# A decode step of attention and an FFN: the first keys on ScalarE's DMA queue, and round 0's product in two pieces

## The chip, the cores and the metric

The kernel runs on one core of a Trainium2 chip. The metric is the device time of one execution in microseconds. The kernel before has a median of 677.2 us over three runs (676.89 to 677.97). All data are float32 and lie in the device's memory (HBM) before the run starts.

## The reference

One decode step for a batch of two. `x` is 2x1x448. The result mixes an attention over a cache of keys and values with a two-layer FFN, by a gate that is computed from `x`:

```
q      = (x @ wq) as 16 heads of 256
scores = q . k_cache / sqrt(256)        # k_cache: 2 x 16 x 4096 x 256
p      = softmax(scores)
a      = (p . v_cache) @ wo             # v_cache: 2 x 16 x 4096 x 256
h      = relu(x @ w1 + b1) ** 2         # 448 -> 1792
b      = h @ w2 + b2                    # 1792 -> 448
g      = sigmoid(sum(x * gate_w))
out    = g * a + (1 - g) * b
```

Keys and values are 134.2 MB each; `wq` and `wo` are 7.3 MB each, `w1` and `w2` together 6.4 MB.

## The kernel before, in words

The work is cut into 16 rounds. A round is a pair of heads of one batch entry: 8.39 MB of keys, laid as 128 partitions of 64 keys x 256 numbers (a row of 64 KB in each partition), and as much of values. In a round VectorE multiplies the keys by the query (in place, line 213), sums over the 256 numbers (line 222) and finds the maxima (223, 224); ScalarE takes the exponentials (240); TensorE multiplies the values by them (`values`, into `po`), sums them (`sums`) and turns the result for the last product with `wo` (`turn`).

Three large buffers in SBUF hold everything that is loaded: `keys[0]`, `keys[1]` and `vals`, 64 KB in each partition. At the start they serve other ends:

- `keys[1]` first receives `wq` with a small pack behind it (`x` transposed, the gate's weights, `b1`). TensorE computes all queries from it (banks `pq`, the semaphore value `TE_Q1` marks that `wq` is read), and only then may the keys of round 1 (k1) be loaded there.
- `keys[0]` receives the keys of round 0 (k0).
- `vals` first receives `wf`, which is `w1` and `w2`. TensorE computes the FFN's first layer from `w1` (into `fin`, then turned into `sm`), VectorE adds the bias, applies the squared relu and multiplies by 1 - g (lines 215 to 218, giving `hT`), and TensorE multiplies `hT` by `w2` into `acc`. The value `TE_ADD` marks that `wf` is read, and only then may the values of round 0 (v0) be loaded into `vals`.

The order of the work is written out by hand, one instruction stream for each engine; semaphores couple them. All big transfers are issued by SyncE (SP), through its one DMA queue, in this order: `wq`, k0, `wf`, k1 (waits for `TE_Q1`), v0 (waits for `TE_ADD`), k2 (waits for round 0's sum on VectorE, since `keys[0]` is then free), v1 (waits for round 0's values on TensorE), and so on in pairs. ScalarE issues one small transfer at the start, the bias `b2` (1.8 KB, line 171). Each round's keys count up the semaphore of their buffer, `KL[0]` or `KL[1]`.

After `wq` has landed, SP has nothing to do with the queries: DVE copies the pack (174), forms the gate's sum, TensorE makes 32 matmuls into the two banks `pq`, ScalarE copies them (182), TensorE spreads them over the partitions and ScalarE copies the eight query tiles `qb` (184). Round 0 of VectorE waits for the first tile.

Of the kernel before, what the change touches and what calls it, by code (L numbers as in the profile page):

```python
# [7 lines left out]
ALU = mybir.AluOpType  # L8
AX = mybir.AxisListType

P = 128
# [23 lines left out]
def gated_mix_kernel(nc, b2, wq, wf, wo, k_cache, v_cache, out):  # L35
    B, H, S, DH = k_cache.shape
# [5 lines left out]
    KEYS = 2 * S // P  # L42
# [11 lines left out]
    pe, dve, act, pool, sp = nc.tensor, nc.vector, nc.scalar, nc.gpsimd, nc.sync  # L54
# [3 lines left out]
    def sb(name, *free):  # L58
        return nc.alloc_sbuf_tensor(name, [P, *free], F32)[:]
# [4 lines left out]
    keys = [sb("k0", PLACE), sb("k1", PLACE)]  # L64
# [29 lines left out]
    DV, AC, TE, GP = (Count(nc, n) for n in ("dve", "act", "pe", "pool"))  # L94
    KL = [Count(nc, "k0_landed"), Count(nc, "k1_landed")]
# [14 lines left out]
    def kv(cache, r):  # L110
        t, b = rounds[r]
        return cache[b, 2 * t:2 * t + 2].rearrange("h (p j) d -> (h p) (j d)", j=KEYS)

    def load(dst, src, sem, after=None):
        ins = sp.dma_start(dst, src)  # L115
        if after:
            after[0].on(ins, after[1])
        return sem.up(ins, 16)
# [10 lines left out]
    def te_mt(r):  # L129
        return TE_MT0 if r == 0 else TE_SUM0 + 4 * (r - 1) + 3  # L130
# [4 lines left out]
    def te_val(r):  # L135
        return TE_SUM0 + 4 * r + 1
# [29 lines left out]


    load(keys[1][:, :3 * N + N // 2 + PK], wq[:, :3 * N + N // 2 + PK], QL)
    load(keys[0], kv(k_cache, 0), KL[0])
    load(vals[:, :spare], wf, FL)  # L170
    BL.up(act.dma_start(b2r, b2), 16)


# [17 lines left out]
    def turned(r):  # L191
        t, b = rounds[r]
        OC.up(TE.on(act.activation(o, po, AF.Copy), te_val(r)))  # L193
        AC_OT[r] = AC.up(TE.on(act.activation(oT[:, t, :, b, :], ot[:, :NJ * 2].rearrange("p (j h) -> p j h", h=2), AF.Copy), te_ot(r)))  # L194

    def normed(r):
        b = rounds[r][1]
        n = DV.up(TE.on(dve.reciprocal(rc, sm[:, :2]), te_sum(r)))
        RL.up(DV.on(dve.scalar_tensor_tensor(rl, rc.unsqueeze(1).to_broadcast([P, 2, 2]), gP[:, 0, b:b + 1],
                                             sel.rearrange("p (s h) -> p s h", s=2), op0=ALU.mult, op1=ALU.mult), n))  # L200

    def k_view(r):
        return keys[r % 2].rearrange("p (j d) -> p j d", d=DH)

    load(keys[1], kv(k_cache, 1), KL[1], (TE, TE_Q1))
    for r, (t, b) in enumerate(rounds):
        kt = k_view(r)
        q = qb[:, (t // 2) * B + b, (t % 2) * DH:(t % 2 + 1) * DH]
        if r < 4:
            dve.wait_ge(AC.h, AC_QB[(t // 2) * B + b])  # L210
        elif r == 4:
            dve.wait_ge(AC.h, AC_QB[-1])
        n = DV.up(KL[r % 2].on(dve.tensor_tensor(kt, kt, q.unsqueeze(1).to_broadcast([P, KEYS, DH]), op=ALU.mult), 16 * (r // 2 + 1)))  # L213
        if r == 0:
            DV_H = DV.up(TE.on(dve.tensor_tensor(hb, sm[:, :FC * B].rearrange("p (c b) -> p c b", b=B), b1T.unsqueeze(2).to_broadcast([P, FC, B]), op=ALU.add), TE_PT))
            DV_H = DV.up(DV.on(dve.tensor_scalar(hb, hb, 0.0, None, op0=ALU.max), DV_H))
            DV_H = DV.up(DV.on(dve.tensor_mul(hT, hb, hb), DV_H))
            DV_H = DV.up(DV.on(dve.tensor_tensor(hT, hT, gP[:, 1, :].unsqueeze(1).to_broadcast([P, FC, B]), op=ALU.mult), DV_H))
            load(vals, kv(v_cache, 0), VL, (TE, TE_ADD))
        else:  # L220
            normed(r - 1)
        DV_S = DV.up(DV.on(dve.tensor_reduce(s, kt, axis=AX.X, op=ALU.add), n))  # L222
        MX.up(DV.on(dve.tensor_reduce(m, s, axis=AX.X, op=ALU.max), DV_S))
        DV_NB = DV.up(TE.on(dve.tensor_reduce(nb, mt[:, :64], axis=AX.X, op=ALU.max, negate=True), te_mt(r)))  # L224
        if r > 0:
            turned(r - 1)
            if r < R - 1:
                load(vals, kv(v_cache, r), VL, (TE, te_val(r - 1)))
            else:
                for i, (lo, hi) in enumerate(zip(WO_CUTS, WO_CUTS[1:])):  # L230
                    load(vals[:, lo * D:hi * D], wo[:, lo * D:hi * D], WL[i], (TE, te_val(r - 1)) if i == 0 else None)
        if r + 2 < R:
            load(keys[r % 2], kv(k_cache, r + 2), KL[r % 2], (DV, DV_S))
        elif r + 2 == R:
            at = V_CUT * DH
            load(keys[r % 2][:, :at], kv(v_cache, R - 1)[:, :at], VT[0], (DV, DV_S))
            load(keys[r % 2][:, at:], kv(v_cache, R - 1)[:, at:], VT[1])
        for hh in range(2):
            z = slice(64 * hh, 64 * hh + 64)
            e = act.activation(p8[z, :, hh:hh + 3:2], s[z].rearrange("p (m s) -> p m s", s=2), AF.Exp,  # L240
                               bias=nb[z], accum_out=rsm[z, hh:hh + 1])
            if hh == 0:
                DV.on(e, DV_NB)
            else:
                EX.up(e)
# [71 lines left out]
    def add(lt, rhs):  # L317
        n = added[0]
        g = 32 * (n % 4)
        added[0] += 1  # L320
        return mm(acc[g:g + B, :D], lt, rhs, n < 4, n >= n_acc - 4)
# [47 lines left out]
    pe.wait_ge(BL.h, 16)  # L369
    pe.wait_ge(DV.h, DV_H)  # L370
    add(gP[0:1, 1, :], b2r)
# [21 lines left out]
    for i, (t, k) in enumerate(blocks):  # L393
# [9 lines left out]
        n = i - early  # L403
# [72 lines left out]
```

## Time and profile before

| | |
|---|---|
| median of three runs | 677.2 us |
| the profiled execution | 676.97 us |
| its span, first to last instruction | 675.6 us |
| bytes read from HBM | 289.55 MB |
| busy: VectorE, TensorE, ScalarE | 566.4 us (84%), 215.6 us (32%), 36.2 us (5%) |
| the data queue's packets | 5772 with 289.56 MB, 99.2% of 16 DMA engines' span |
| mean granted TensorE clock | 0.653 |

The page shows one profiled execution. "Span" is the time from its first to its last instruction, and the profiled execution's own time has 1.4 us around it. The share of the DMA queue is the time that its packets took on the core's 16 DMA engines, as a share of the span. A row of the timeline gives the start in us, the duration, the engine (SPq and ACTq are the engines' own sequencers, here issuing DMAs), the line, the operation with its tile and the number of instructions merged into it, and in brackets the idle time before it with what ended it. In the names, `k` stands for either keys buffer, `v` for `vals`.

### The profile page before, as it was taken

To read this page: it belongs to the slowest core of one execution; us is meant where nothing else is said; L and a number is where in the kernel's file an instruction comes from. 1 tells how busy PE (TensorE), PEld (TensorE's weight loads), DVE (VectorE), ACT (ScalarE), POOL (GpSimd) and SP (SyncE) were. 2 spreads that over 40 slices of the span, in tenths; PEclk is the share of its full clock that TensorE was granted. 3 is DMA by queue.
4 is the path that set the end of the run, shared out by engine and by line. 5 is a ranking of instruction groups with operands and counts; after the bars stand their busy time and mean duration, and the time that the engine had idled before them with its cause. 6 is when DMAs were issued, how large, how long until landed. Compare 5 with 4: busy or idle time off the path is not lost. (4 is left out here: it accounts for less than half of the span.)

```text
span 675.6 us, 3473 instructions
## 1 busy us (share of the span) xinstructions
PE 215.6 (32%) x1522; PEld 67.6 (10%) x1522; DVE 566.4 (84%) x120; ACT 36.2 (5%) x111; POOL 2.1 (0%) x15
## 2 busy tenths in 40 slices
PE   0726141150605124060503305050421405051357
PEld 0201000010101101010100101010010101011012
DVE  1066999999989797998979798997979799797960
ACT  0121000000000000000000000000000000000000
POOL 1000000000000000000000000000000000000000
PEclk9976666575756657585755658575565858565579
DMA  9999999999999999999999999999999999999997
GB/s 381 431 453 421 435 435 436 435 431 435 435 435 435 435 431 435 435 435 435 435 435 435 435 435 435 431 435 435 435 431 435 435 435 435 435 435 435 423 418 293
DMA packets 5779, 289.63 MB, mean 429 GB/s; under 512 B 653, under 2 KB 782, under 8 KB 1038
## 3 DMA queue, kind: packets, MB, share of 16 engines
q1 hardware_dynamic: 5772, 289.56, 99.2%
q8 instruction: 3, 0.05, 0.0%
q14 instruction: 2, 0.02, 0.0%
q10 hardware_dynamic: 2, 0.00, 0.0%
HBM read 289.55 MB, written 0.00 MB: 429 GB/s over the span
## 5 line engine op out<-in xcount | busy, mean ns | idle before, releaser
L213 DVE TENSOR_TENSOR k<-k,q 128x16384 f32<-128x16384 f32 x16 | 275.6, 17223 | 51.7 <-DMA k<-in_k_cache_dram 51.7
L222 DVE TENSOR_REDUCE s<-k 128x64 f32<-128x16384 f32 x16 | 275.4, 17212 | 0.0
L274 PE MATMUL po<-v,p 128*4 128x512 f32 x960 | 137.4, 737 | 291.4 <-PEq L278 291.4
L274 PEld LDWEIGHTS po<-v,p 128*4 128x4 f32 x960 | 26.6, 99 | 389.5 <-issue 389.5
L274 PE MATMUL mt<-ident,m 128*64 128x64 f32 x64 | 7.7, 334 | 88.8 <-PEq L278 88.8
L193 ACT ACTIVATE o<-po 128x512 f32<-128x512 f32 x16 | 9.6, 597 | 449.8 <-PE po L274 449.8
L274 PE MATMUL ot<-rl,o 128*128 128x2 f32 x128 | 16.4, 250 | 15.6 <-PEq L278 15.6
L274 PEld LDWEIGHTS ot<-rl,o 128*128 128x128 f32 x128 | 15.5, 191 | 30.0 <-issue 30.0
L240 ACT ACTIVATE p<-s,nb 64x64 f32<-64x64 f32 x32 | 11.2, 350 | 104.8 <-DVE nb L224 104.6
L274 PE MATMUL sm<-rsm,ones 128*128 128x2 f32 x32 | 8.9, 348 | 21.2 <-PEq L278 21.2
L274 PEld LDWEIGHTS mt<-ident,m 128*64 128x64 f32 x64 | 5.2, 205 | 90.4 <-issue 90.4
L174 DVE COPY pk<-k 128x28 f32<-128x28 f32 x1 | 0.2, 179 | 16.5 <-DMA k<-in_wq_dram 16.5
L224 DVE TENSOR_REDUCE nb<-mt 128x1 f32<-128x64 f32 x16 | 3.6, 224 | 10.6 <-PE mt L274 10.6
L274 PE MATMUL fin<-v,pk 128*2 128x448 f32 x32 | 6.0, 933 | 16.6 <-DMA v<-in_wf_dram 16.6
L274 PEld LDWEIGHTS sm<-rsm,ones 128*128 128x128 f32 x32 | 8.0, 310 | 23.8 <-issue 23.8
L258 DVE COPY wide<-oT 128x2 f32<-128x2 f32 x8 | 0.7, 162 | 10.4 <-ACT oT L194 10.4
L274 PE MATMUL pq<-k,pk 128*2 128x512 f32 x64 | 9.3, 747 | 0.0
L274 PE MATMUL po<-k,p 128*4 128x512 f32 x64 | 8.7, 702 | 0.0
L274 PE MATMUL sm<-ys,ones 128*128 128x2 f32 x2 | 0.6, 350 | 21.0 <-DVE ys L177 21.0
L261 DVE COPY y<-fin 128x112 f32<-128x112 f32 x1 | 0.3, 275 | 7.7 <-PE fin L274 7.7
L240 ACT ACTIVATION_READ_ACCUMULATOR p<-s,nb 64x1 f32 x32 | 5.9, 184 | 0.0
L274 PE MATMUL acc<-v,oT 128*2 128x448 f32 x48 | 4.9, 538 | 0.4 <-ACT oT L194 0.3
(59 smaller groups left out, 58.2 us busy)
## 6 DMA issues: line engine op xcount, KB each, us to landing
k<-in_wq_dram SPq DMA_DIRECT2D x1, 7182.0 KB, 19.6
v<-in_wf_dram SPq DMA_DIRECT2D x1, 6272.0 KB, 52.8
k<-in_v_cache_dram SPq DMA_DIRECT2D x1, 6144.0 KB, 37.8
v<-in_wo_dram SPq DMA_DIRECT2D x1, 3584.0 KB, 18.6
k<-in_v_cache_dram SPq DMA_DIRECT2D x1, 2048.0 KB, 42.4
v<-in_wo_dram SPq DMA_DIRECT2D x1, 1792.0 KB, 22.6
v<-in_wo_dram SPq DMA_DIRECT2D x1, 896.0 KB, 24.3
v<-in_wo_dram SPq DMA_DIRECT2D x1, 672.0 KB, 25.4
```

The lines of the kernel that those rows point to most:

```text
L174: DV_PK = DV.up(QL.on(dve.tensor_copy(pk, keys[1][:, 3 * N + N // 2:3 * N + N // 2 + PK]), 16))
L193: OC.up(TE.on(act.activation(o, po, AF.Copy), te_val(r)))
L213: n = DV.up(KL[r % 2].on(dve.tensor_tensor(kt, kt, q.unsqueeze(1).to_broadcast([P, KEYS, DH]), op=ALU.mult), 16 * (r // 2 + 1)))
L222: DV_S = DV.up(DV.on(dve.tensor_reduce(s, kt, axis=AX.X, op=ALU.add), n))
L224: DV_NB = DV.up(TE.on(dve.tensor_reduce(nb, mt[:, :64], axis=AX.X, op=ALU.max, negate=True), te_mt(r)))
L240: e = act.activation(p8[z, :, hh:hh + 3:2], s[z].rearrange("p (m s) -> p m s", s=2), AF.Exp, bias=nb[z], accum_out=rsm[z, hh:hh + 1])
L258: DV_W = dve.tensor_copy(wide[:, n, 0:W:16], o_block(t, k))
L261: DV_Y4 = DV.up(TE.on(dve.tensor_copy(y4, fin[:, :DQ]), TE_FIN))
L274: return pe.matmul(dst, lt, rhs, start=start, stop=stop)
```

## The change

Two edits. The first takes k0's load from SP's queue and has ScalarE issue it, ahead of the transfer of `b2`; SP issues `wq` and behind it at once `wf`. The second cuts round 0's product (the multiplication of the keys by the query) in two: 48 of the 64 keys of each partition, then the four steps of the FFN's first layer, then the other 16 keys. Rounds 1 to 15 keep their product in one piece. Semaphores and what they count stay as they were.

```
-    load(keys[0], kv(k_cache, 0), KL[0])
     load(vals[:, :spare], wf, FL)
+    KL[0].up(act.dma_start(keys[0], kv(k_cache, 0)), 16)
     BL.up(act.dma_start(b2r, b2), 16)
...
-        n = DV.up(KL[r % 2].on(dve.tensor_tensor(kt, kt, q.unsqueeze(1).to_broadcast([P, KEYS, DH]), op=ALU.mult), 16 * (r // 2 + 1)))
+        cut = 48 if r == 0 else KEYS
+
+        def times_q(lo, hi):
+            return DV.up(KL[r % 2].on(dve.tensor_tensor(kt[:, lo:hi], kt[:, lo:hi], q.unsqueeze(1).to_broadcast([P, hi - lo, DH]), op=ALU.mult), 16 * (r // 2 + 1)))
+
+        n = times_q(0, cut)
         if r == 0:
             DV_H = DV.up(TE.on(dve.tensor_tensor(hb, sm[:, :FC * B].rearrange("p (c b) -> p c b", b=B), b1T.unsqueeze(2).to_broadcast([P, FC, B]), op=ALU.add), TE_PT))
             DV_H = DV.up(DV.on(dve.tensor_scalar(hb, hb, 0.0, None, op0=ALU.max), DV_H))
             DV_H = DV.up(DV.on(dve.tensor_mul(hT, hb, hb), DV_H))
             DV_H = DV.up(DV.on(dve.tensor_tensor(hT, hT, gP[:, 1, :].unsqueeze(1).to_broadcast([P, FC, B]), op=ALU.mult), DV_H))
+            n = times_q(cut, KEYS)
             load(vals, kv(v_cache, 0), VL, (TE, TE_ADD))
```

Two places in the order of instructions change. The first is the start of SP's stream, which is the order of its DMA queue (`in_wq`, `in_wf` and the caches are the sources; `pe` and `dve` are the engines whose semaphores a row waits for). Before, and then with the change:

```order
L115 DMA k<-in_wq_dram 128x14364 [waits barrier_Pool_Activation_PE_DVE_SP_release]
L115 DMA k<-in_k_cache_dram 128x16384
L115 DMA v<-in_wf_dram 128x12544
L115 DMA k<-in_k_cache_dram 128x16384 [waits pe]
L115 DMA v<-in_v_cache_dram 128x16384 [waits pe]
```

```order
L115 DMA k<-in_wq_dram 128x14364 [waits barrier_Pool_Activation_PE_DVE_SP_release]
L115 DMA v<-in_wf_dram 128x12544
L115 DMA k<-in_k_cache_dram 128x16384 [waits pe]
L115 DMA v<-in_v_cache_dram 128x16384 [waits pe]
L115 DMA k<-in_k_cache_dram 128x16384 [waits dve]
```

The second row of before, k0, is gone from SP's stream. It now stands at the head of ScalarE's, where `b2` was first, ahead of the load of the activation table. The other place is round 0 on VectorE (`k` is the keys buffer, `hb` and `hT` the FFN's hidden layer, `s` the scores). Before, and then with the change:

```order
L213 TENSOR_TENSOR k<-k,q 128x16384 [waits act,k0_landed]
L215 TENSOR_TENSOR hb<-sm,pk 128x28 [waits pe]
L216 TENSOR_SCALAR hb<-hb 128x28 [waits dve]
L217 TENSOR_TENSOR hT<-hb 128x28 [waits dve]
L218 TENSOR_TENSOR hT<-hT,gP 128x28 [waits dve]
L222 TENSOR_REDUCE s<-k 128x64 [waits dve]
```

```order
L216 TENSOR_TENSOR k<-k,q 128x12288 [waits act,k0_landed]
L220 TENSOR_TENSOR hb<-sm,pk 128x28 [waits pe]
L221 TENSOR_SCALAR hb<-hb 128x28 [waits dve]
L222 TENSOR_TENSOR hT<-hb 128x28 [waits dve]
L223 TENSOR_TENSOR hT<-hT,gP 128x28 [waits dve]
L216 TENSOR_TENSOR k<-k,q 128x4096 [waits k0_landed]
L228 TENSOR_REDUCE s<-k 128x64 [waits dve]
```

A quarter of the product now stands behind the four steps of the FFN and ahead of the sum.

## Prediction

> **What bounds the kernel now.** I read the page's DMA rows first, then the chain that ended last, then the rounds in the timeline, then the first 95 us.
>
> ```profile
> q1 hardware_dynamic: 5772, 289.56, 99.2%
> q8 instruction: 3, 0.05, 0.0%
> q14 instruction: 2, 0.02, 0.0%
> ...
> DMA 4%; PE 2%; SPq 0%; DVE 0%; issue 0%
> ```
>
> One queue carries all the data, and its packets fill 99.2% of the sixteen DMA engines' span. The chain that ended last is short and names a transfer as its longest part. VectorE's 84% looks like a bound, so the rounds must decide. Two of them late in the run:
>
> ```profile
> 558.99 8.54 PE L274 MATMUL po<-v,p 128*4 128x512 f32 x64 [20.70 <-PEq L278]
> ...
> 578.23 17.23 DVE L213 TENSOR_TENSOR k<-k,q 128x16384 f32<-128x16384 f32 x1 [2.86 <-DMA k<-in_k_cache_dram]
> ...
> 597.68 9.67 PE L274 MATMUL po<-v,p 128*4 128x512 f32 x64 [20.69 <-PEq L278]
> ...
> 616.93 17.22 DVE L213 TENSOR_TENSOR k<-k,q 128x16384 f32<-128x16384 f32 x1 [2.87 <-DMA k<-in_k_cache_dram]
> ```
>
> A round takes 616.93 - 578.23 = 38.70 us. Keys and values of a round are 16.78 MB, so 433 GB/s. VectorE idles 2.87 us in each, for the keys to land; it could do a round in 35.8. So the end is set by bytes in the queue. The change moves no byte more or less: it can only alter the time by making the queue start earlier, run at another rate, or run empty.
>
> The first 95 us hold everything that moves:
>
> ```profile
> 0.73 0.51 ACTq L171 DMA_DIRECT2D b2r<-in_b_dram  x1
> ...
> 0.74 0.39 SPq L115 DMA_DIRECT2D k<-in_wq_dram  x1
> ...
> 1.19 0.41 SPq L115 DMA_DIRECT2D k<-in_k_cache_dram  x1
> ...
> 1.64 0.43 SPq L115 DMA_DIRECT2D v<-in_wf_dram  x1
> ...
> 20.31 0.18 DVE L174 COPY pk<-k 128x28 f32<-128x28 f32 x1 [16.48 <-DMA k<-in_wq_dram]
> ...
> 30.92 0.33 SPq L115 DMA_DIRECT2D k<-in_k_cache_dram  x1
> ...
> 31.94 0.60 ACT L184 ACTIVATE q<-ot 128x512 f32<-128x512 f32 x1 [0.42 <-PE ot L274]
> ...
> 36.03 1.88 PE L274 MATMUL pq<-v 128*128 128x512 f32 x4
> ...
> 39.63 17.23 DVE L213 TENSOR_TENSOR k<-k,q 128x16384 f32<-128x16384 f32 x1 [17.63 <-DMA k<-in_k_cache_dram]
> ...
> 54.48 6.05 PE L274 MATMUL fin<-v,pk 128*2 128x448 f32 x32 [16.56 <-DMA v<-in_wf_dram]
> ...
> 62.30 0.19 DVE L215 TENSOR_TENSOR hb<-sm,pk 128x28 f32<-128x28 f32 x1 [5.44 <-PE sm L274]
> ...
> 62.95 0.19 DVE L218 TENSOR_TENSOR hT<-hT,gP 128x28 f32<-128x28 f32 x1
> 63.06 17.21 DVE L222 TENSOR_REDUCE s<-k 128x64 f32<-128x16384 f32 x1
> ...
> 68.99 0.33 SPq L115 DMA_DIRECT2D v<-in_v_cache_dram  x1
> 80.30 0.33 SPq L115 DMA_DIRECT2D k<-in_k_cache_dram  x1
> ...
> 81.33 17.21 DVE L213 TENSOR_TENSOR k<-k,q 128x16384 f32<-128x16384 f32 x1
> ...
> 94.32 8.77 PE L274 MATMUL po<-v,p 128*4 128x512 f32 x64 [11.29 <-PEq L278]
> ...
> 117.07 17.21 DVE L213 TENSOR_TENSOR k<-k,q 128x16384 f32<-128x16384 f32 x1
> ```
>
> The landings stand one behind the other: wq 20.3, k0 39.6, wf 54.5, v0 94.3. Each later issue is ahead of need: k1 leaves at 30.92, v0 at 68.99, k2 at 80.30. When a new transfer's packets begin, the fine windows of the same trace show (the last column is GB/s; sixteen packets begin together, so a burst marks the begin of a row on most engines):
>
> ```profile
> 1.00:1.60 0.60, 0.00 (x0) 0.00 (x0) 0.54 (x2) 0.32 (x1) 0.50 (x2) 1.00 0.00 0
> 1.60:2.60 1.00, 0.00 (x0) 0.00 (x0) 0.89 (x3) 0.96 (x1) 1.00 (x8) 1.00 2.70 921
> ...
> 53.20:54.20 1.00, 0.00 (x0) 0.00 (x0) 1.00 (x1) 0.00 (x0) 0.00 (x0) 0.50 2.43 1049
> 54.40:58.00 3.60, 3.52 (x20) 0.69 (x24) 2.46 (x1) 0.00 (x0) 0.00 (x0) 0.50 0.67 291
> ...
> 70.20:70.80 0.60, 0.00 (x0) 0.00 (x0) 0.60 (x1) 0.00 (x0) 0.00 (x0) 1.00 3.53 1529
> 72.60:73.20 0.60, 0.00 (x0) 0.00 (x0) 0.60 (x1) 0.00 (x0) 0.00 (x0) 1.00 3.54 1529
> 75.00:75.60 0.60, 0.00 (x0) 0.00 (x0) 0.60 (x1) 0.00 (x0) 0.00 (x0) 0.50 3.27 1420
> ```
>
> The first data flow 0.9 to 1.9 us after the issue at 0.74: that is the lead a transfer needs. A row of keys (64 KB) takes 2.4 us on an engine, 70.2 to 72.6 to 75.0. Eight rows make a transfer (128 partitions on 16 engines), so k1's rows begin at 53.2 to 54.2 and v0's at 72.6 to 73.2, both without a gap.
>
> **The change part by part.**
>
> *k0 on ScalarE's queue.* Now wq and k0 are in flight together. No row shows two data queues at once, so I bound the time W at which wq lands. From below it is 20.3, if k0 takes nothing from it; from above 39.6, when before both had landed. A fair share puts wq near the upper end, so I work with 39.6, the dearest: 19.3 us later than before. Everything that hangs on wq moves by 19.3.
>
> k1's issue: 30.92 + 19.3 = 50.2, data 51.1 to 52.1. Its place begins at 53.2. Cost 0, with 1.1 us to spare; wf's bytes, which SP has queued behind wq, are the cover. Without wf, the queue would lie empty from 39.6 to about 51.6, 12 us.
>
> [...]
>
> *The product in two pieces.* The first query tile is ready at 31.94 + 0.60 + 19.3 = 51.8. By then k0 is there. 48 of 64 keys take 17.23 x 48/64 = 12.9 us, to 64.8. TensorE ends its query work at 36.03 + 1.88 + 19.3 = 57.2; wf has landed by 54.5; `fin` takes 6.05, then 62.30 - 60.53 = 1.8 us to the bias: 65.0. So both arrive together, 65.0, where before it was 62.3. The four steps take 62.95 + 0.19 - 62.30 = 0.84, to 65.9. From there to v0's issue before: 68.99 - 63.14 = 5.85, now 71.7. Data flow from 72.6 to 73.6, where they were needed at 72.6 to 73.2: cost 0 to 1.0 us. I take 0, since W = 39.6 was the dearest case. Here the cut is the cover: in one piece the product would end at 69.0, v0 be issued at 75.7 and the engines stand idle for 3.4 to 5 us.
>
> *TensorE's clock.* The first layer ran at a granted clock of 0.50 (54.40 to 58.00 in the windows), 17 us after the query work. [...]
>
> *The second piece and what is late next.* 4.3 us behind the steps: 70.2, sum to 87.4, so k2 leaves at 87.4 instead of 80.30. Its data follow v0's eight rows, 72.6 + 8 x 2.41 = 91.9 at the earliest, and need up to 1.9 us of lead: 2.6 us to spare. The exponentials of round 0 are 7.1 us later too, at 88.5, while v0 lands at 94.3. VectorE needs 117.07 - 81.33 = 35.74 for a round where the queue needs 38.70, so the 7.1 us are gone after three rounds. Splitting adds one instruction, off the path.
>
> *ScalarE's order.* One issue more ahead of `b2` and the table load, some 0.4 to 0.5 us at 0.7, where ScalarE then waits for wq; b2, now behind k0, is wanted at 65.9. Both 0.
>
> *The rate.* While both queues run, from 2 to 38 us, the rate may differ. Above: wq's 7.35 MB landed at 20.3, and at the 433 GB/s of the rounds they take 17.0; of the 3.3 us at the start, 0.74 precede the issue and 0.9 the first data, so at most 1.6 can be won by a second queue that fills gaps. Below, the slowest stretch of these is that of k0, 420 GB/s:
>
> ```profile
> 20.20:39.60 19.40, 16.88 (x82) 5.16 (x82) 0.68 (x4) 6.15 (x11) 0.00 (x0) 1.00 0.97 420
> ...
> 54.40:94.20 39.80, 13.80 (x78) 3.69 (x78) 33.56 (x9) 2.70 (x6) 0.00 (x0) 0.63 0.98 422
> 94.20:132.90 38.70, 10.83 (x78) 3.52 (x78) 37.97 (x7) 1.65 (x6) 0.00 (x0) 0.63 1.00 434
> ```
>
> 420 for 434 over 36 us is 1.2 us. (The 39.80 us for k1 and v0, 1.1 more than a round, are no price of the short lead: the bursts at 70.2, 72.6 and 75.0 are unbroken. I put them down to the few packets of the instruction queues in the first rows.) Nearest is the row of k0 alone: 0.
>
> Sum: 676.97 + 0 + 0 + 0 = 677.0 for the profiled execution, bounds -1.6 and +1.0 + 1.2. The profiled execution lies 0.2 under the median, so I say 677.1.
>
> **The rivals.**
>
> *The start is filled better.* For it: 3.3 us pass before the rate is full, and one late engine costs 1.1 behind wf. Against it: the same sixteen engines work, and neither issue is earlier than 0.73. All of the 1.6 gives 675.6; with the 1.1 gone too, 674.5.
>
> *The query chain comes too late.* The mechanism: sharing costs rate, so wq lands after 39.6, and SP, which issues in order, holds k1 and behind it v0. k1's place is at 53.2 and the chain from W to its data 10.6 + 1.9 us, so it decides from W = 40.7. With the 1.2 us of rate, which put W at 40.8, and the 1.0 of v0 that is 679.3; each further us of W adds one.
>
> *The transfers do not mix.* One queue may be served first. If wq, the start is as before but for k2 at 62.95 + 0.19 + 4.3 + 17.2 = 84.7, still ahead of 91.9; if k0, W is 39.6 and the sum above holds. Either way 677.1.
>
> **How the numbers follow.** A measurement of this kernel tells 0.2%, 1.4 us, from no change. No effect by the full queue: 0.60; the transfers do not mix: 0.06; better start: 0.15, of which I count all as faster; query chain too late: 0.19, slower. Faster 0.15, same 0.66, slower 0.19. The range, 675.4 to 679.3, reaches the full gain of the start and the price of the late chain.
>
> **What would show it.** Right: wq's copy (line 174) begins at 37 to 40, k1 leaves at 48 to 50.5, v0 before 72, and bursts at 2.4 us steps run through 53 and 73; the values of round 0 still begin at about 94.3, and the rounds stay at 38.70. Wrong: a stretch without packets near 52 or 73, values of round 0 later than 95.5, or a landing of wf well off 54.5. A change of the rounds' 38.70 would break the argument as a whole.

## The result, and the profile after

The change makes the kernel slower: 678.6 us median over 22 runs (677.33 to 679.94) against 677.14 us for the kernel before, run beside it as often (676.76 to 678.24). The ratio is 1.0019, with a 95% interval of 1.0013 to 1.0025, so 1.3 us, 0.9 to 1.7 (it goes by all the runs; the two medians lie 1.46 us apart). The forecast was no change.

From the page of the changed kernel, the second DMA queue and the chain that ended last:

```profile
q10 hardware_dynamic: 146, 8.39, 2.9%
...
DMA v<-in_wo_dram 4%; PE po L280 1%; PE fin L280 0%; SPq L115 0%; DVE y L267 0%
```

The second queue carries k0's 8.39 MB and the end is still a chain behind a transfer. The bound has not moved, so I looked for a time in which the queue moved nothing. The start of its timeline:

```profile
39.60 0.18 DVE L174 COPY pk<-k 128x28 f32<-128x28 f32 x1 [35.78 <-DMA k<-in_wq_dram]
...
50.15 0.33 SPq L115 DMA_DIRECT2D k<-in_k_cache_dram  x1
...
51.87 12.96 DVE L216 TENSOR_TENSOR k<-k,q 128x12288 f32<-128x12288 f32 x1 [10.58 <-ACT q L184]
...
57.08 3.19 PE L280 MATMUL fin<-v,pk 128*2 128x448 f32 x32
...
60.93 1.05 PE L280 MATMUL sm<-ident,o 128*128 128x8 f32 x10 [0.66 <-ACT o L186]
64.75 0.18 DVE L220 TENSOR_TENSOR hb<-sm,pk 128x28 f32<-128x28 f32 x1
...
65.40 0.19 DVE L223 TENSOR_TENSOR hT<-hT,gP 128x28 f32<-128x28 f32 x1
...
65.73 1.65 PE L280 MATMUL acc<-b2r,gP 1*2 1x448 f32 x2 [3.76 <-DVE hT L223]
...
67.31 5.80 PE L280 MATMUL acc<-v,hT 128*2 128x448 f32 x28
...
73.16 0.33 SPq L115 DMA_DIRECT2D v<-in_v_cache_dram  x1
...
94.99 9.49 PE L280 MATMUL po<-v,p 128*4 128x512 f32 x64 [5.04 <-PEq L284]
```

wq lands at 39.6, k1 leaves at 50.15, round 0's product starts at 51.87: all as forecast. The view of the DMA issues gives the time from issue to landing (last column):

```profile
k<-in_wq_dram SPq DMA_DIRECT2D x1, 7182.0 KB, 38.8
k<-in_k_cache_dram ACTq DMA_DIRECT2D x1, 39.1
```

wq and k0 were issued together and landed 0.3 us apart, so the two shared the engines and neither was served first. v0 leaves at 73.16 and not at 71.7. Fine windows of the same trace show what that does (the third column from the right is the granted TensorE clock, the last GB/s):

```profile
53.20:54.20 1.00, 1.00 (x4) 0.49 (x3) 1.00 (x1) 0.74 (x2) 0.00 (x0) 1.00 2.43 1049
55.60:56.60 1.00, 1.00 (x4) 0.38 (x2) 1.00 (x1) 0.74 (x2) 0.00 (x0) 1.00 2.42 1049
71.80:72.60 0.80, 0.80 (x8) 0.08 (x2) 0.80 (x1) 0.00 (x0) 0.00 (x0) 0.50 0.20 82
72.60:73.40 0.80, 0.51 (x4) 0.00 (x0) 0.80 (x1) 0.00 (x0) 0.00 (x0) 0.97 0.01 0
...
74.00:74.80 0.80, 0.00 (x0) 0.00 (x0) 0.80 (x1) 0.00 (x0) 0.00 (x0) 1.00 3.78 1311
76.80:77.60 0.80, 0.00 (x0) 0.00 (x0) 0.80 (x1) 0.00 (x0) 0.00 (x0) 0.50 3.02 1311
62.00:65.60 3.60, 0.00 (x0) 0.00 (x0) 3.50 (x6) 0.17 (x1) 0.00 (x0) 0.56 0.92 400
62.40:62.60 0.20, 0.00 (x0) 0.00 (x0) 0.20 (x1) 0.00 (x0) 0.00 (x0) 0.51 0.00 0
65.60:73.20 7.60, 7.38 (x30) 1.08 (x30) 7.57 (x2) 0.00 (x0) 0.00 (x0) 0.54 0.86 371
```

k1's rows begin at 53.2 and again 2.4 us later: no gap there. But v0's rows, which began at 72.6 to 73.2 before, begin at 74.0 to 74.8, with no row in the window from 72.6 to 73.4. That is a hole of 1.4 us, and the next row follows after 2.8 us instead of 2.4, so the refill costs some 0.4 more. The last three rows show why v0 was late. TensorE had nothing to do from 62.0 to 65.7, its granted clock fell to 0.50 at 62.4 (0.56 on the mean of that time), and it computed the FFN's second layer at 0.54 on the mean, in 7.4 us; the clock was back only at 72.6, when the layer was all but done.

The hole stays to the end. The values of round 1 and of round 14, in the kernel before and then in the changed one:

```profile
133.27 9.77 PE L274 MATMUL po<-v,p 128*4 128x512 f32 x64 [14.49 <-PEq L278]
...
636.41 9.09 PE L274 MATMUL po<-v,p 128*4 128x512 f32 x64 [20.72 <-PEq L278]
```

```profile
134.91 8.30 PE L280 MATMUL po<-v,p 128*4 128x512 f32 x64 [9.22 <-PEq L284]
...
638.04 9.32 PE L280 MATMUL po<-v,p 128*4 128x512 f32 x64 [20.70 <-PEq L284]
```

1.64 us later in round 1, 1.63 in round 14: no round gives any of it back or adds to it. The profiled execution took 678.82 us, 1.85 more than that of before.

### The profile page after: what moved, and what is told of

The parts are those of the page before. It is cut to its first block, busy times and chain, and to the rows that moved or that the text cites. A ratio compares the mean times of both kernels' runs of the same rounds, so it can differ in the third digit from the quotient of the medians.

```text
span 677.5 us, 3474 instructions
## 1 busy us (share of the span) xinstructions
PE 216.7 (32%) x1522; PEld 67.7 (10%) x1522; DVE 566.4 (84%) x121; ACT 36.1 (5%) x111; POOL 2.1 (0%) x15
## 3 DMA queue, kind: packets, MB, share of 16 engines
q10 hardware_dynamic: 146, 8.39, 2.9%
## 5 line engine op out<-in xcount | busy, mean ns | idle before, releaser
L216 DVE TENSOR_TENSOR k<-k,q 128x16384 f32<-128x16384 f32 (+2 forms) x17 | 275.7, 16219 | 39.5 <-DMA k<-in_k_cache_dram 28.9
L280 PE MATMUL po<-v,p 128*4 128x512 f32 x960 | 139.6, 746 | 266.8 <-PEq L284 266.8
L280 PE MATMUL acc<-v,hT 128*2 128x448 f32 x28 | 5.8, 923 | 0.0
## 6 DMA issues: line engine op xcount, KB each, us to landing
v<-in_wf_dram SPq DMA_DIRECT2D x1, 6272.0 KB, 53.2
```

Of the source, the lines that this page charges most:

```text
L216: return DV.up(KL[r % 2].on(dve.tensor_tensor(kt[:, lo:hi], kt[:, lo:hi], q.unsqueeze(1).to_broadcast([P, hi - lo, DH]), op=ALU.mult), 16 ...
L280: return pe.matmul(dst, lt, rhs, start=start, stop=stop)
```

## The experiments

The theory after reading the trace: v0 is issued after the queue has run empty, since the FFN's steps wait for 48 keys of product that start 12 us later, and since TensorE's clock falls meanwhile. Rivals: two queues cost by themselves; the cut costs by itself; the second layer is slow because of what runs beside it. All times are in us; each ratio is to the kernel before run in the same session, with its 95% interval. e1 has five runs, e5 four, the others eleven. Those runs of the kernel before had a median of 677.12 in the first session, 677.59 in the second and 678.02 in the third.

| run | median (range) | ratio to before |
|---|---|---|
| e1, queue only | 682.1 (681.46 to 683.61) | 1.0072 (1.0058 to 1.0086) |
| e2, cut only | 676.96 (676.78 to 678.02) | 0.9993 (0.9984 to 1.0002) |
| e3, cut at 32 | 677.68 (676.83 to 678.51) | 1.0004 (0.9995 to 1.0013) |
| e4, TensorE kept busy | 677.71 (676.78 to 678.94) | 1.0008 (0.9999 to 1.0017) |
| e5, cut at 56 | 680.26 (679.97 to 680.81) | 1.0044 (1.0029 to 1.0060) |
| e6, before, end kept busy | 677.1 (676.88 to 677.43) | 0.9996 (0.9987 to 1.0005) |
| e7, e4 with e6's edit | 677.29 (676.83 to 678.18) | 0.9996 (0.9987 to 1.0005) |
| e8, the change with e6's edit | 678.71 (677.04 to 679.22) | 1.0014 (1.0005 to 1.0023) |
| e9, e7 with k1 later | 678.94 (678.37 to 679.98) | 1.0015 (1.0006 to 1.0025) |
| e10, e7 with early matmuls | 677.68 (677.10 to 677.99) | 1.0000 (0.9991 to 1.0009) |

### e1: the queue alone

```
-        cut = 48 if r == 0 else KEYS
+        cut = KEYS
...
-            n = times_q(cut, KEYS)
```

> The first edit alone: k0 on ScalarE's queue, round 0's product in one piece. Theory (v0 is issued too late and the DMA queue runs empty): the product runs from 51.9 to 69.1, the FFN's steps to 70.0, its second layer at half clock 7.6 us, v0's issue at 77.5, first data at 78.4 instead of 72.7: a hole of 5.7 us and 0.6 for the refill, so 677.1 + 6 = about 683 us. Rival (sharing the DMA engines between two queues costs by itself, the product's cut does nothing): 678.6.

```profile
69.52 1.65 PE L279 MATMUL acc<-b2r,gP 1*2 1x448 f32 x2 [8.02 <-DVE hT L223]
...
76.25 0.33 SPq L115 DMA_DIRECT2D v<-in_v_cache_dram  x1
```

682.1, where the theory had 683 and the rival 678.6. In the timeline TensorE waits 8.02 us for the FFN's steps, v0 leaves at 76.25. Without the cut the first edit costs 5 us; the cut buys most of it back.

### e2: the cut alone

```
     load(keys[1][:, :3 * N + N // 2 + PK], wq[:, :3 * N + N // 2 + PK], QL)
+    load(keys[0], kv(k_cache, 0), KL[0])
     load(vals[:, :spare], wf, FL)
-    KL[0].up(act.dma_start(keys[0], kv(k_cache, 0)), 16)
```

> The second edit alone: k0 back on SP's queue between wq and wf, the product cut at 48. Theory: v0's issue stays at 69.0, since the FFN's first layer waits for wf and not for the product; k2 leaves at 84.7, still ahead of its place at 92: 677.1, no change. Rival (the cut costs by itself, or the later k2 does): about 678.6.

```profile
69.34 0.33 SPq L115 DMA_DIRECT2D v<-in_v_cache_dram  x1
83.72 0.33 SPq L115 DMA_DIRECT2D k<-in_k_cache_dram  x1
...
94.25 9.49 PE L280 MATMUL po<-v,p 128*4 128x512 f32 x64 [7.79 <-PEq L284]
```

No change, as the theory said. The later k2 (83.72 for 80.30) costs nothing, and v0's values begin at 94.25 (94.32 before).

### e3: the cut after 32 keys

```
-        cut = 48 if r == 0 else KEYS
+        cut = 32 if r == 0 else KEYS
```

> The changed kernel with the cut after 32 keys instead of 48. Theory: the first piece ends at 51.9 + 8.7 = 60.6, before the first layer is done at 62.0, so the FFN's steps run from 62.0 to 62.9; TensorE has idled about 1 us and keeps its clock, the second layer takes 3.5 to 4.2 us, v0's issue at 66.4 to 67.1, no hole at 73: 677.1. Rival (two queues cost by themselves): 678.6.

```profile
62.19 0.91 PE L280 MATMUL acc<-b2r,gP 1*2 1x448 f32 x2 [1.04 <-DVE hT L223]
...
63.02 4.87 PE L280 MATMUL acc<-v,hT 128*2 128x448 f32 x28
...
67.94 0.33 SPq L115 DMA_DIRECT2D v<-in_v_cache_dram  x1
```

The first piece is done at 59.7, VectorE waits for the first layer and not the other way round, TensorE idles 1.04 us ahead of the second, v0 leaves at 67.94 and the loss is gone, to within the measurement. k0 is still on ScalarE's queue. The second layer took 5.8 us, more than my 3.5 to 4.2: a pause of 1.04 us did not keep the clock, which stood at 0.71 on the mean from 62.2 to 68.0.

### e4: the cut at 48, TensorE kept busy

```
     done(ins, TE_PT)
+    for n in range(16):
+        g = 32 * (n % 4)
+        mm(pq[0][g:g + B, :D], xT[:, 0, :], vals[:, (n % 4) * D:(n % 4 + 1) * D])
     pe.wait_ge(BL.h, 16)
```

> The changed kernel, cut at 48, with sixteen extra matmuls behind the first layer, whose results go unused, so that TensorE does not idle from 62.0 to 65.7. Theory (the half clock after that idle time is what made v0 late): the second layer takes 3.5 to 4.2 us instead of 7.5, v0's issue at 69.1 to 69.8 instead of 73.2, no hole: 677.1. Rival (the second layer is slow because it runs beside VectorE's multiplication and the loads): it stays at 7.5 us, v0's issue at 73.2, 678.6.

```profile
60.93 3.19 PE L280 MATMUL pq<-v,pk 128*2 128x448 f32 x32
...
64.75 0.91 PE L280 MATMUL acc<-b2r,gP 1*2 1x448 f32 x2 [0.64 <-DVE hT L223]
...
65.59 3.17 PE L280 MATMUL acc<-v,hT 128*2 128x448 f32 x28
...
68.81 0.33 SPq L115 DMA_DIRECT2D v<-in_v_cache_dram  x1
```

```profile
64.60:68.80 4.20, 4.01 (x30) 0.82 (x30) 4.20 (x2) 0.00 (x0) 0.00 (x0) 1.00 1.15 499
72.60:73.40 0.80, 0.00 (x0) 0.00 (x0) 0.80 (x1) 0.00 (x0) 0.00 (x0) 1.00 2.84 1229
```

This run decides between the causes of the slow second layer. VectorE multiplies beside it as in the changed kernel, and the loads run; only TensorE's idle time is filled. The clock stays at 1.00, the layer takes 4.0 us instead of 7.4, and v0's rows begin at 72.6 as before. From the end of the FFN's steps to v0's issue it is 4.2 us here and in the profiles of e7, e9 and e10, which have the same sixteen matmuls. The time returns to 677.71, level with before as far as the interval tells.

### e5: a larger dose

```
-        cut = 48 if r == 0 else KEYS
+        cut = 56 if r == 0 else KEYS
```

> The changed kernel with the cut after 56 keys instead of 48: a dose. Theory (v0's lateness is paid one for one once the queue is empty): the first piece ends 2.15 us later, the second layer is at half clock again, v0's issue at about 75.3 in place of 73.2, and the time 2.1 us above the changed kernel's 678.6: 680.7. Rival (the cost is one of sharing, or of the second queue): 678.6.

```profile
74.49 0.33 SPq L115 DMA_DIRECT2D v<-in_v_cache_dram  x1
```

Between the profiled executions of the change, e5 and e1, v0 leaves at 73.16, 74.49 and 76.25, and they took 678.82, 680.18 and 681.80: steps of 1.33 and 1.76 in the issue, 1.36 and 1.62 in the time. Once the queue was empty, lateness was paid about one for one. v0 left 0.8 us before the 75.3 that I expected, since the layer did not run as long at half clock (its groups of weight loads are 0.75 us apart up to 72.56 and 0.38 from 73.15 on): 6.45 us from its first matmul to v0's issue, for 7.43 in the changed kernel.

### e6, e7, e8: the end kept busy

The profiled execution of e2 took 677.56 although its rounds ran level with before. Its end and that of the kernel before:

```profile
666.00:668.00 2.00, 2.00 (x12) 0.30 (x9) 0.54 (x8) 0.00 (x0) 0.00 (x0) 0.50 0.96 401
```

```profile
666.00:668.00 2.00, 2.00 (x28) 0.52 (x20) 0.00 (x0) 0.00 (x0) 0.00 (x0) 1.00 0.93 387
```

In e2 TensorE fell to 0.50 just ahead of the products with `wo`, after a pause of 0.97 us and small matmuls, and they took 6.32 us:

```profile
665.90 6.32 PE L280 MATMUL acc<-v,oT 128*2 128x448 f32 x48 [0.26 <-ACT oT L194]
```

The 22 runs of the kernel before lie in two groups, twelve at 676.76 to 677.20 and ten at 677.59 to 678.24. To see whether that is this clock, e6 fills the pause in the kernel before, e8 in the changed kernel and e7 in e4:

```
+    for n in range(4):
+        mm(pq[0][32 * n:32 * n + B, :], xT[:, 0, :], keys[R % 2][:, n * QB:(n + 1) * QB])
     done(turn(), te_ot(R - 1))
```

> The kernel before with four extra matmuls, whose results go unused, between the last values and the last turn, where TensorE idles about 1 us. Theory (the runs of before lie in two groups, near 676.8 and near 677.9, because TensorE sometimes drops to half clock between 664 and 670 us, as in the profile of the cut alone): the upper group vanishes, all runs at 676.7 to 677.0. Rival (the groups come from the transfers): two groups as before, median 677.1.

> The changed kernel with TensorE kept busy in both places: sixteen extra matmuls behind the first layer and four ahead of the last turn. If two queues cost nothing by themselves and the end's clock is the only noise left: 676.8, level with the kernel before that has the four. If sharing has a price of its own, some tenths more: 677.1 to 677.4.

> The changed kernel with the four extra matmuls ahead of the last turn only. Theory (two causes: v0's late issue at the start, the clock at the end): the start's cost stays, 1.0 to 1.7 us above the kernel before that has the four, so 677.8 to 678.5, and the runs spread less than the changed kernel's 677.3 to 679.9. Rival (the changed kernel's cost sits at the end): 676.8.

```profile
663.48 1.03 PE L274 MATMUL pq<-k,pk 128*2 128x512 f32 x8
...
665.91 4.69 PE L274 MATMUL acc<-v,oT 128*2 128x448 f32 x48 [0.26 <-ACT oT L194]
```

In e6's profile the products with `wo` begin at 665.91, as in e2, and take 4.69 us. Its eleven runs lie within 676.88 to 677.43: the upper group is gone, though they reach 0.4 above what I expected. The interval of its ratio still contains 1, so it isn't shown to beat the kernel before. e8 is at 678.71, 1.6 above e6: the loss sits at the start, not at the end. e7 and e8 ran side by side and differ only in the sixteen matmuls of e4: 677.29 with them, 678.71 without.

The profile of e6 holds more. Its start is that of the kernel before, and so is the pause of TensorE ahead of the FFN's second layer (1.04 us there, 1.03 in the first profile). Its rows, and the clock of the kernel before from 63.2 to 69.0:

```profile
62.15 1.65 PE L274 MATMUL acc<-b2r,gP 1*2 1x448 f32 x2 [1.04 <-DVE hT L218]
...
69.27 0.33 SPq L115 DMA_DIRECT2D v<-in_v_cache_dram  x1
```

```profile
63.20:69.00 5.80, 5.66 (x30) 0.94 (x30) 5.80 (x1) 0.00 (x0) 0.00 (x0) 0.71 1.15 497
```

From the end of the FFN's steps to v0's issue this execution took 7.26 us, where the kernel before took 5.85 in its own profile. In e6 the second layer's groups of weight loads begin 0.75 us apart to the end, at 68.17; in the kernel before they do so up to 66.68 and are 0.37 to 0.38 apart from 67.28 on, where the clock, down to 0.50 from 63.71 to 67.12, was back at 1.00. So this stretch differs by 1.4 us between executions of the same instructions. With the pause of 3.7 us it took 7.57 in the changed kernel and 6.18 in e8. In these profiles the layer is slow where the clock is down, and for how long it is down differs from one to the next: 3.41 us in the kernel before and e3, 6.83 in e2 (61.66 to 68.49), 10.24 in the changed kernel (62.40 to 72.64), by windows of 0.1 and 0.2 us around the second layer.

e8's runs spread nearly as far as the changed kernel's, so the end's clock is not all that varies. e7, at 677.29, falls in the case of a price for sharing, but e6 itself came out at 677.1 and not 676.8, 0.2 below e7, and the two ratios are equal: whether two queues have a small price of their own stays open. The profile of e8 holds a hint:

```profile
50.81 0.33 SPq L115 DMA_DIRECT2D k<-in_k_cache_dram  x1
```

```profile
53.20:54.20 1.00, 1.00 (x3) 0.38 (x2) 1.00 (x1) 0.68 (x2) 0.00 (x0) 1.00 2.27 786
54.20:55.20 1.00, 1.00 (x4) 0.52 (x3) 1.00 (x1) 0.60 (x1) 0.00 (x0) 1.00 0.72 262
55.60:56.60 1.00, 1.00 (x4) 0.46 (x3) 1.00 (x1) 0.74 (x2) 0.00 (x0) 1.00 0.46 197
56.60:57.60 1.00, 1.00 (x3) 0.19 (x1) 1.00 (x1) 0.71 (x2) 0.00 (x0) 1.00 1.66 721
```

k1 left at 50.81, and here its rows don't begin together: 12 rows (786 GB/s for 1 us, 64 KB each) by 54.2 and four behind it, and of the second rows only three begin from 55.6 to 56.6 (197 GB/s), where sixteen do in the changed kernel (1049). v0 then left earlier than in the changed kernel's profile (72.42 for 73.16), yet the values of round 0 begin later (96.35 for 94.99), so in this execution a part of the loss arose ahead of v0, most likely at k1's late rows; how large a part isn't separated. k1's issue lies between 49.17 and 50.81 in the profiles of the change, e1, e3, e4, e5, e7 and e8. It follows the length of the query matmuls, which take 8.34 us in e4, 9.27 in the change and 9.88 in e8: their groups of four weight loads come 0.85 us apart at first and 0.43 later, and the closer ones begin at another time in each execution (43.78 in e4, 45.62 in the change, 46.70 in e8).

### e9 and e10: k1 later, k1 earlier

Both start from e7.

```
     wqt = keys[1]
+    for n in range(16):
+        g = 32 * (n % 4)
+        mm(mt[g:g + B, :], xT[:, 0, :], wqt[:, n * QB:(n + 1) * QB])
```

> The changed kernel with TensorE busy in both places (the kernel of 677.3 us), and sixteen more unused matmuls ahead of the queries, so that wq is read about 1.7 us later and k1 leaves at 51 to 52.5. Theory (k1's place in the queue is at 53.2 and it needs 2.4 to 3 us of lead, so the query chain that hangs on wq has no slack left): a hole near 53, 1 to 1.7 us and 0.6 for the refill: 678.5 to 679.5. Rival (the lead needed is the 0.9 to 1.9 us of the first transfer): at most 0.6 more, 677.3 to 677.9.

```profile
54.05 0.33 SPq L115 DMA_DIRECT2D k<-in_k_cache_dram  x1
```

The dose was larger than meant: the matmuls took 6.4 us, k1 left at 54.05, after its place. The ratio is 1.0015, where e7's was 0.9996, so a late k1 costs too; but with an issue past the place both readings of the lead would give a loss: k1's part of the run doesn't tell how much lead is needed. v0's part of it does to some extent. It left at 73.68, only 1.3 us ahead of its place at 75.0, and its rows began there, by the later bursts: those at 80.0 to 92.4 come in steps of 2.4 us, which lead back to 75.2, and the values of round 0 begin at 95.64.

```
+    for n in range(150):
+        mm(mt[:, :P], ident, ident)
     pe.wait_ge(DV.h, DV_YS)
```

> The kernel of 677.3 us with TensorE kept busy on the identity until wq lands (150 unused matmuls), so that the queries run at full clock from their start and k1 leaves 2 to 3 us earlier, at 47 to 48. Theory (what is left of the changed kernel's cost is k1's issue, too late in some executions): level with the kernel before that has the four matmuls at the end, 676.9 to 677.1, and the runs lie closer together. Rival (two queues cost some tenths by themselves): 677.3 as without.

```profile
40.91 0.18 DVE L174 COPY pk<-k 128x28 f32<-128x28 f32 x1 [37.08 <-DMA k<-in_wq_dram]
...
50.61 0.33 SPq L115 DMA_DIRECT2D k<-in_k_cache_dram  x1
```

This run missed its aim. wq landed at 40.91 instead of 39.5, k1 left at 50.61 and not at 47 to 48, so it says nothing on an early k1. What delayed wq was not shown. The 150 matmuls, which ran from 2.82 to 38.80, also ended 2.7 us before TensorE's next work, and the queries' groups of weight loads again came 0.85 us apart at first and 0.43 from 45.22 on, so the queries didn't start at their full speed either.

## Why the prediction was wrong

**The bound** held: bytes in the queue, 38.70 us for a round before and after. So did the three ways in which the change could act; it acted by the third, a queue that ran empty.

**W and k1.** wq landed at 39.6, the upper bound that I worked with; k1 left at 50.15 (50.2 forecast) and the rows at 53 ran on. The 37 us from which wq's copy was expected is shown by no run: the copy began at 39.47 to 39.66 in the change, e1, e3 to e5 and e7 to e9, and at 40.91 in e10. Whether the 1.1 us to spare were real is open. e8's rows had already spread with an issue at 50.81, 2.4 us ahead of 53.2, but e9's v0, issued 1.3 us ahead of its place, began without a gap.

**The product in two pieces** is where the prediction failed, at one term of the sum: "From there to v0's issue before: 5.85, now 71.7." It measured 73.16 - 65.59 = 7.57, and so v0 was issued 1.5 us later than forecast, after its place at 72.6. I took the duration of the second layer from one execution and treated it as fixed. In that execution the clock rose in mid-layer (0.71 on the mean from 63.2 to 69.0); in e6's the same instructions at the same place took 7.26. The longer idle time, 3.76 us for 1.03, is therefore not needed for such a duration, and the 7.57 of one profile is partly chance: e1, e5 and e8, with TensorE idle for 3.7 to 8.0 us, took 6.87, 6.59 and 6.18. The half clock was in the prediction's own windows (0.50 behind an idle time of 16.56 us), and e4 shows that it is the cause: with the idle time filled, a clock of 1.00, 4.0 us for the layer and no loss beyond the interval.

**TensorE's clock.** The sum took `fin` at 6.05 us, its time at a clock of 0.50; it took 3.19, at 1.00 (57.0 to 60.2). But `fin` was not what the steps waited for. VectorE came to them at 64.75, whatever TensorE did, and the 3 us saved became idle time. In it the clock fell, 0.4 us after TensorE's last matmul, and it came back 6.9 us after the second layer began: 0.56 on the mean of the idle time, 0.54 on that of the layer. In the four profiles whose windows show the whole of such a stretch around the second layer, the clock stayed down for 3.41 us (the kernel before, e3), 6.83 (e2) and 10.24 (the change), which is once, twice and three times 3.41; what sets the number wasn't shown. By the rows alone I had TensorE and VectorE arriving together at 65.0; TensorE was done at 61.98.

**The hole's price.** 0 to 1.0 was stated, and 0 taken with the reason that 39.6 was the dearest case for wq. It was the actual case. At 73.16 the hole measured 1.4 us and the refill of the queue, which had no term, some 0.4 more. The direction of the doubt was plain from this: apart from the clock, every unknown in that part could only add. (The last step of the sum is off as well: 677.0 and 0.2 up to the median are 677.2, not 677.1.)

**The rivals.** The rival on the slower side named v0's issue as its second term and had 679.3, with wq later than 40.7 as its condition. wq came in time; the price came from the part behind it. That one queue is served first, the third rival, is ruled out by the landings of wq and k0, 0.3 us apart. The better start did not come: the first slice of the page has 403 GB/s for 381, but k1's rows begin at 53.2 as before.

**What stays open:** whether two queues cost some tenths by themselves. e3, e4 and e7 contain no change in their intervals; a k1 that is late in some executions, as in e8, would explain the upper runs, and so would a second layer that is slow in some; neither e9 nor e10 tested that.

## What to carry to other kernels

This kernel, bound by transfers, lost time where a transfer's issue came after the queue was empty, and there about one for one: with v0's issue later by 1.33 and 1.76 us the time grew by 1.36 and 1.62 (the change, e5, e1). So list each issue with the time at which its place in the queue begins, and treat a slack of one or two microseconds as doubtful: the same instructions ahead of v0's issue took 5.85 us in one execution and 7.26 in another. When work is moved, don't carry along a TensorE duration that was read in one execution: look whether the granted clock was up or down in it, and what the same stretch took in other executions. The first layer got faster ahead of a wait (3.19 us for 6.05), and that only lengthened the idle time behind it (3.76 for 1.03). Where a cut makes room for a chain, let the chain's producer set it (32 keys here, so that VectorE waits), not the share that looks balanced on paper.

## What the runs showed of the hardware that was not expected

The two groups of run times of the kernel before, 0.4 to 1.5 us apart, come from TensorE's clock in the last ten microseconds: four unused matmuls in a pause of 1 us made them one (e6, 676.88 to 677.43). No upper run of the kernel before was itself profiled; that the clock falls there is seen in e2's profile. A pause of 0.97 us with small matmuls around it was enough for a drop to 0.50 in one execution (e2) and not in another (the changed kernel, 1.00 from 666 to 672). Around the FFN's second layer the clock stayed down for 3.41 us in the profile of the kernel before and for 6.83 in e2's, with the same matmuls there and the same pause of 1.03 us.

In the changed kernel the first row on the empty DMA queue took 2.8 us to the next one (bursts at 74.0 and 76.8), where rows of the same size follow each other in 2.4 (53.2 and 55.6). And one row begins late at 59.2 to 59.6, behind its burst (328 GB/s in a window of 0.2 us, 64 KB), in the traces of the kernel before, the change, e1 to e5 and e7, whatever ran there; what it is stays open.
